# Loading the first batch's keys and queries as six consecutive rows of a head, and transposing them on two corners of the TensorE array

## The chip, the cores and the metric

The kernel runs on one core of a Trainium2 chip. The metric is the device time of one execution in microseconds (us). A core has TensorE (matrix products, PE in the profile, its weight loads PEld), VectorE (DVE), ScalarE (ACT), GpSimd (POOL) and SyncE (SP, which here only issues transfers), and 16 DMA engines that move data between the device memory and the on-chip memory. The on-chip memory has 128 partitions; what TensorE reads or writes also lies across partitions.

## The reference

Attention over 4 batches, 8 heads, 768 positions and 64 elements a head, with two kinds of heads, and then a feed-forward layer on its result.

```python
scores = scale * np.matmul(q, k.transpose(0, 1, 3, 2))      # q, k: (4, 8, 768, 64), float32
causal = rel >= 0                                           # rel = query position - key position
stream_keep = causal & (is_sink | in_win)                   # first 4 keys, or a window of 64
mask = np.where(retr, full_mask, stream_mask)               # retrieval heads 0, 2, 6: all earlier keys
a = softmax(np.where(mask, scores, -1e9))
attn = np.matmul(a, v)                                      # then to x: (3072, 512)
h = np.maximum(np.maximum(x @ w1, x @ w2), x @ w3)          # w: (512, 768)
return h @ w_out                                            # (768, 512)
```

## The kernel before

The order of all the work is written out by hand: `PROGRAM` (L84 to L150) is a list of small steps, and each engine carries out its instructions in the order in which these steps issue them. An engine whose next instruction waits holds up everything behind it.

The work goes by batch and, within one, by halves of 384 positions. For each half there are scores (a matrix product of keys and queries into PSUM, then the exponential on ACT into `pt`), masks, the product with the values (`av`), a turn of the result (`xT`), the hidden layer (`f`, L439) and the output (`o`, L464). Batches 1 to 3 take their keys and queries by GpSimd loads that cast on the way (`load`, L261) and turn them with VectorE (L275). Batch 0 is different, and it alone is touched by the change. Its path is:

- `load_pairs` (L198): one transfer for the keys and one for the queries of a pair of heads and a half of the positions, 192 KB each, as float32. There are four pairs and two halves, so 16 transfers. Partition p takes rows 3p to 3p + 2 of both heads of the pair: 3 x 64 floats of a head are 768 consecutive bytes. `hl` steps call it, and the first two pairs are loaded ahead of the program (L314, L315). SP issues 13 of the transfers, ACT 3.
- `cast_pair` (L216, step `cast`): a cast to float16 for the keys (`kn`) and one for the queries (`qn`), by the engine that the step names (d is VectorE, a ScalarE, p GpSimd). It also changes the order from head-row-element to row-head-element.
- `turn_pair` (L228, step `turnp`): TensorE transposes the 128 x 128 block of each j (row in a partition's three) into a PSUM bank `tr`, three for the keys and three for the queries. One or two copies (L241) bring them into `KQ`, sorted by position; head 0 of the pair lies on partitions 0 to 63, head 1 on 64 to 127.
- `first_scores` (L589, step `s0`) uses `KQ`.

The queues around it. SP issues its transfers in order, and from the ninth on a transfer waits for the landing of the one eight before it, since there are eight completion counters (DMAHW0 to 7) for the transfers of SP and ACT together. The staging buffers of three of the groups of pairs (`pairs2`) are two deep, so the third group also waits for casts of the first. The program's lines that bear on the order:

```python
"idle 11, hl 0 2 2 s cs, cast 0 1 pd, turnp 0 1 aa, cast 0 0 dd, cast 0 2 dp, load_v 0 0 0 4 s",
"s0 0 0 3, vc 0 0 4 p, vc 0 4 4 p, s0 0 0 1, kx0 0 2 p, s0 0 0 2, hl 1 2 2 s s, cast 1 0 dd",
"turnp 1 0 dd, load 1 0 0, cast 1 1 pp, w 0, load 1 0 1, cast 1 3 dp, vt 0 02 da, cast 1 2 aa",
"vt 0 1 a, turnp 1 1 d, y 0 0 1:4:2 r p, s0 0 1 2, s0 0 1 3, y 0 0 4:5:1 r r, turnp 1 3 ad",
```

In `load 1 0 0` and `load 1 0 1` GpSimd issues the keys and queries of batch 1, in `w 0` the first weight matrix (L400).

Of the kernel before, what the change touches and what calls it, by code (L numbers as in the profile page):

```python
# [9 lines left out]
FP16 = mybir.dt.float16  # L10
FP32 = mybir.dt.float32
# [5 lines left out]
PAIRS = ((0, 2), (1, 3), (4, 6), (5, 7))  # L17
# [136 lines left out]
def fast(ctx, tc, keep, q, k, v, is_retrieval, n_sink, window, moe_w1, moe_w2, moe_w3, moe_w_out, w_t, woutt, out):  # L154
    nc = tc.nc
    B, H, S, D = q.shape
    DMdl = out.shape[1]
    DF = moe_w1.shape[1]
    P = 128
# [4 lines left out]
    HALF = S // 2  # L164
    HB = HALF // P
# [9 lines left out]
    pairs2 = ctx.enter_context(tc.tile_pool(name="pairs2", bufs=2))  # L175
    once = ctx.enter_context(tc.tile_pool(name="once", bufs=1))
    third = ctx.enter_context(tc.tile_pool(name="third", bufs=2))
    half16 = ctx.enter_context(tc.tile_pool(name="half16", bufs=3))
# [11 lines left out]
    def bank(shape, dtype, name):  # L190
        return bkp.tile(shape, dtype, tag="bank", name=name)
# [4 lines left out]
    staged, cast, KQs, landed = {}, {}, {}, {}  # L196

    def load_pairs(half, hp, n, engines):  # L198
        for nm, src, eng in zip(("ks", "qs"), (k, q), engines):
            st = (  # L200
                pairs2.tile([P, 4, HB, D], FP32, tag=nm, name=nm) if n == 2
                else once.tile([P, 2 * n, HB, D], FP32, name=f"{nm}{hp}")
            )
            for h in range(0, 2 * n, 2):
                h0, h1 = PAIRS[hp + h // 2]
                eng[h // 2].dma_start(  # L206
                    out=st[:, h : h + 2],
                    in_=src[0, h0 : h1 + 1 : h1 - h0, half * HALF : (half + 1) * HALF].rearrange(
                        "h (p j) d -> p h j d", p=P
                    ),  # L210
                )
            for i in range(n):
                staged.setdefault((half, hp + i), []).append(st[:, 2 * i : 2 * i + 2])
                landed[half, hp + i] = st[0:1, 2 * i, 0, 0:2]

    def cast_pair(half, hp, engines):  # L216
        cast[half, hp] = []
        for nm, src, op in zip(("kn", "qn"), staged.pop((half, hp)), engines):
            x = half16.tile([P, HB, 2, D], FP16, tag=nm, name=nm)
            op(out=x, in_=src.rearrange("p h j d -> p j h d"))  # L220
            cast[half, hp].append(x)

    def of_pair(hp):
        return KQs[0, hp // 2].rearrange("p i t two -> p i (t two)")[
            :, hp % 2
        ].rearrange("p (i t) -> p i t", i=2)

    def turn_pair(half, hp, *engines):  # L228
        if (0, hp // 2) not in KQs:
            KQs[0, hp // 2] = qkt.tile([P, 2, S, 2], FP16, tag="KQ", name="KQ")  # L230
        xs = cast.pop((half, hp))
        n = 2 // len(engines)
        for part, op in enumerate(engines):
            tr = bank([P, 1024], FP16, "tr")
            for i in range(n):
                for j in range(HB):
                    c = i * HALF + j * P
                    nc.tensor.transpose(
                        tr[:, c : c + P], xs[part + i][:, j].rearrange("p h d -> p (h d)"), ident
                    )  # L240
            op(  # L241
                out=of_pair(hp)[
                    :, part : part + n, half * HALF : (half + 1) * HALF
                ].rearrange("p i (t j) -> p i t j", j=HB),
                in_=tr[:, 0 : n * HALF].rearrange("p (i j t) -> p i t j", i=n, j=HB),
            )

    def load(b, quad, *which):
# [61 lines left out]
    def load_first(half, hp, n, *e):  # L310
        by = {"s": nc.sync, "c": nc.scalar}
        load_pairs(half, hp, n, [[by[x] for x in y * n][:n] for y in e])
# [10 lines left out]
    def idle_work(n):  # L323
# [11 lines left out]
        out=kb[:, 2:4], in_=kb[:, 2:4], compare_op=ALU.is_ge, fill=0.0,  # L335
# [3 lines left out]
        out=kb[:, 3], in_=kb[:, 3], compare_op=ALU.is_gt, fill=0.0,  # L339
# [3 lines left out]
        out=kb[:, 1:5:3], in_=kb[:, 1:5:3], compare_op=ALU.is_gt, fill=0.0,  # L343
        base=window - P, pattern=[[0, 2], [-1, P]], channel_multiplier=1,
    )
    ident = consts.tile([P, P], FP16, name="ident")
# [4 lines left out]
        out=every3, in_=every3, compare_op=ALU.not_equal, fill=1.0,  # L351
# [4 lines left out]
    if n_sink > 0:  # L356
# [4 lines left out]
        out=far, in0=kb[:, 0:5], scalar1=FAR, scalar2=-FAR, op0=ALU.mult, op1=ALU.add  # L361
# [346 lines left out]
    xs = {}  # L708
# [35 lines left out]
    def turn_x(b, half, hp, op):  # L744
        x = xs.pop((b, half, hp))
        tr = bank([P, 1024], FP16, "tr")
        for i in range(HB):
            nc.tensor.transpose(  # L748
                tr[:, i * P : (i + 1) * P], x[:, i].rearrange("p h d -> p (h d)"), ident
            )  # L750
        op(out=xT[b, half, hp].rearrange("p a t -> p (a t)"), in_=tr[:, 0:HALF])
# [55 lines left out]
    def reduce_one(out, in_):  # L807
# [12 lines left out]
        f=lambda b, half, wi, ni, *e: hidden(int(b), int(half), int(wi), int(ni), *[ops[x] for x in e]),  # L820
# [7 lines left out]
        x=lambda b, half, hp, e: turn_x(int(b), int(half), int(hp), ops[e]),  # L828
# [223 lines left out]
```

## Time and profile before

| | us |
|---|---|
| median of 3 runs | 187.92 (187.65 to 189.06) |
| the profiled execution | 187.55 |
| its span, first to last instruction | 186.1 |
| PE, DVE, ACT, POOL busy in the span | 178.6, 144.9, 99.4, 82.8 |
| PE busy in the first 30 us | 27.6 (the 2 us rows of the windows view, added) |

The profile's times are those of one execution. A matmul's end is modelled, so that short matmuls issued back to back overlap in the rows; their spacing is read from a group's length. The DMA share of a window is the mean over 16 engines, and can pass 1 a little where packets overlap. A row of the timeline gives the start, the duration, the engine, the line, the operation, what it writes and reads, and how many of the kind stand together.

### The profile page before, as it was taken

Reading aid. Unit: us, or ns where it says so; the run is one execution under the profiler, and the core shown is the slowest. Engines: PE = TensorE matmul, PEld = TensorE weight load, DVE = VectorE, ACT = ScalarE, POOL = GpSimd, SP = SyncE. Lnnn points to the kernel's source line nnn. Section 1 sums busy time; section 2 is a strip of 40 time slices with the busy share of each in tenths; the row PEclk is TensorE's granted clock in tenths of the full one; section 3 lists DMA queues with packets and bytes.
Section 4 is the critical chain, followed back from the end, with each engine's and each line's share of the span. In section 5 each row is a group of like instructions: output and inputs, shape, how many; then the busy total and the mean of one; then the engine's idle time right before and its main releaser. Section 6 shows DMA issues by size and latency. Waiting matters only on the chain.

```text
span 186.1 us, 4755 instructions
## 1 busy us (share of the span) xinstructions
PE 178.6 (96%) x1863; PEld 105.5 (57%) x1863; DVE 144.9 (78%) x308; ACT 99.4 (53%) x161; POOL 82.8 (44%) x142
## 2 busy tenths in 40 slices
PE   6889999999999999999999999999999999999992
PEld 2455646566656456765555566655655575555551
DVE  3659997989899977888979899765883699475553
ACT  3399998378955648687096336665446301311110
POOL 7498998809883990299057002126313400000000
PEclk9999999999999999999999999999999999999999
DMA  5999999999899999349593301321133013401404
GB/s 157 318 328 291 212 209 209 212 236 220 165 143 163 170 269 212 79 105 221 142 258 90 113 0 56 67 81 56 27 65 113 0 60 63 139 2 56 167 19 161
DMA packets 43005, 26.30 MB, mean 141 GB/s; under 512 B 29794, under 2 KB 38498, under 8 KB 42978
## 3 DMA queue, kind: packets, MB, share of 16 engines
q1 hardware_dynamic: 37826, 17.44, 36.4%
q0 software_dynamic: 4192, 7.87, 23.3%
q10 hardware_dynamic: 960, 0.66, 1.2%
q8 instruction: 15, 0.25, 0.5%
q14 instruction: 12, 0.10, 0.2%
HBM read 25.17 MB, written 6.29 MB: 169 GB/s over the span
## 4 chain that ended last, share of the span: by engine, by line
PE 85%; DVE 7%; DMA 3%; ACT 2%; SPq 1%; issue 1%; DVEq 0%; ACTq 0%
PE yy L439 47%; PE yy L464 15%; PE oacc L725 8%; PE st L682 7%; PE yst L439 3%; DMA qs<-in_q_dram 3%; DVE KQ L241 2%; PE yst L464 1%; DVE KQ L275 1%; SPq L206 1%; ACT pt L637 1%; DVE x L732 1%; DVE vx L808 1%; PE st L616 1%; PE vb L513 1%; PE tr L748 1%
## 5 line engine op out<-in xcount | busy, mean ns | idle before, releaser
L379 POOL TENSOR_TENSOR pt<-pt,kb 128x512 f16<-128x512 f16 (+5 forms) x53 | 48.3, 932 | 59.3 <-ACT pt L699 50.4
L699 ACT ACTIVATE pt<-st 128x1024 f16<-128x1024 f32 (+2 forms) x51 | 43.5, 908 | 24.9 <-PE st L682 24.5
L439 PE MATMUL yy<-xT,w2t 128*128 128x384 f16 x184 | 36.2, 326 | 0.0
L439 PE MATMUL yy<-xT,w0t 128*128 128x384 f16 x180 | 34.5, 326 | 0.0
L439 PE MATMUL yy<-xT,w1t 128*128 128x384 f16 x176 | 34.2, 326 | 0.0
L464 PE MATMUL yy<-woutt,hT 128*128 128x512 f16 (+1 forms) x138 | 31.4, 372 | 0.0
L451 DVE TENSOR_TENSOR hT<-yy,acc 128x384 f16<-128x384 f32 x46 | 25.2, 556 | 5.0 <-PE yy L439 3.3
L451 DVE TENSOR_TENSOR acc<-yy,acc 128x384 f16<-128x384 f32 x44 | 24.0, 556 | 5.8 <-PE yy L439 4.2
L275 DVE STREAM_TRANSPOSE KQ<-kq 128x384 f32<-128x384 f32 x24 | 25.3, 1132 | 1.0 <-POOL pt L379 1.0
L439 PEld LDWEIGHTS <-w0t 128*128 128x128 f16 x192 | 18.1, 98 | 12.5 <-issue 0.4
L447 ACT CAST acc<-yy 128x384 f16<-128x384 f32 x27 | 12.9, 491 | 22.7 <-PE yy L439 20.6
L439 PEld LDWEIGHTS <-w1t 128*128 128x128 f16 x192 | 17.8, 98 | 11.9 <-issue 0.6
L439 PEld LDWEIGHTS <-w2t 128*128 128x128 f16 x192 | 17.7, 98 | 11.8 <-issue 0.2
L464 PEld LDWEIGHTS <-hT 128*128 128x128 f16 x150 | 14.4, 98 | 15.3
L473 ACT COPY ot<-yy 128x512 f32<-128x512 f32 (+1 forms) x14 | 7.9, 566 | 21.4 <-PE yy L464 18.9
L725 PEld LDWEIGHTS <-pt 128*128 128x128 f16 x472 | 17.2, 97 | 3.6 <-issue 0.6
L725 PE MATMUL oacc<-va,pt 128*128 128x65 f16 x392 | 18.6, 193 | 0.2 <-DVE pt L379 0.2
L732 DVE TENSOR_TENSOR x<-oacc,sums 128x384 f16<-128x384 f32 x32 | 17.8, 558 | 1.1
L637 ACT ACTIVATE pt<-st 128x1024 f16<-128x1024 f32 (+5 forms) x22 | 15.4, 767 | 0.4 <-PE st L616 0.2
L682 PE MATMUL st<-KQ 32*128 32x128 f16 (+2 forms) x342 | 15.1, 257 | 0.0
L379 DVE TENSOR_TENSOR pt<-pt,kb 128x256 f16<-128x256 f16 (+4 forms) x31 | 12.3, 401 | 1.8 <-ACT pt L699 1.7
L447 DVE CAST acc<-yy 128x384 f16<-128x384 f32 x18 | 10.0, 559 | 3.4 <-PE yy L439 3.0
(119 smaller groups left out, 190.7 us busy)
## 6 DMA issues: line engine op xcount, KB each, us to landing
out_dram<-ot SPq DMA_DIRECT2D x23, 256.0 KB, 2.0
vs<-in_v_dram SPq DMA_DIRECT2D x18, 256.0 KB, 4.9
ks<-in_k_dram SPq DMA_DIRECT2D x8, 192.0 KB, 5.9
kq<-in_k_dram POOLq DMA_DIRECT2D x3, 384.0 KB, 7.7
kq<-in_q_dram POOLq DMA_DIRECT2D x3, 384.0 KB, 9.3
qs<-in_q_dram SPq DMA_DIRECT2D x5, 192.0 KB, 5.4
kq<-in_k_dram POOLq DMA_DIRECT2D x3, 288.0 KB, 6.0
kq<-in_q_dram POOLq DMA_DIRECT2D x3, 288.0 KB, 7.1
```

What stands on the lines that cost most here:

```text
L275: nc.vector.transpose(out=dst.rearrange("c (p j) -> c j p", j=n)[:, j0:j1], in_=src.rearrange("c (j i) -> c j i", i=R),)
L379: engine.tensor_tensor(out=x, in0=x, in1=of_blocks(kb, pattern, rows), op=ALU.mult)
L439: nc.tensor.matmul(yy[:, 0:HALF], w_t[wi][:, ks, ni * P : (ni + 1) * P], xT[b, half, ks].rearrange("p a t -> p (a t)"), start=(ks == 0), s ...
L447: op(out=acc[b, half, ni], in_=yy[:, 0:HALF])
L451: nc.vector.tensor_tensor(out=acc[b, half, ni] if wi == 1 else hT[b, half, ni], in0=yy[:, 0:HALF], in1=acc[b, half, ni], op=ALU.max,)
L464: nc.tensor.matmul(yo[:, 0:n], hT[b, half, ns][:, tb * P : (tb + 1) * P], woutt[:, ns, c : c + n], start=(ns == 0), stop=(ns == NNB - 1),)
L473: op(out=ot[:, c : c + n], in_=yo[:, 0:n])
L637: nc.scalar.activation(out=pts[0, half, hp, u][:, r0:r1, c0:c1], in_=sts[hp][:, r0:r1, c0:c1], func=AF.Exp, scale=sc,)
L682: nc.tensor.matmul(sts["XY"[g // 2]][:, g % 2, c0 : c0 + n * P], KQ[rows, 0, ki * P : (ki + 1) * P] if kind == "p" else kx[b % 2][quad][ro ...
L699: nc.scalar.activation(out=pts[b, s, xy][:, r0:r1, c0:c1], in_=st[:, r0:r1, c0:c1], func=AF.Exp, scale=sc,)
L725: nc.tensor.matmul(o[:, i, r, 0 : D + 1], at[b, h, kind, ki, qi], vv[:, 0 : D + 1], start=(n == 0), stop=(n == len(todo) - 1), skip_group_ ...
L732: nc.vector.tensor_tensor(out=x, in0=o[:, :, :, 0:D], in1=rc.unsqueeze(3).to_broadcast([P, HB, 2, D]), op=ALU.mult,)
```

## The change

The transfer now gives a head of the pair to each half of the partitions. Partition p of the lower half takes rows 6p to 6p + 5 of the first head, and partition 64 + p those of the second, so that 6 x 64 floats, 1536 consecutive bytes, are one piece. The number of transfers, their bytes, their order and the issuing engines stay. The source pattern now has the head outermost, then 64 groups of rows, then 384 floats: `h p (j d)` in place of `p h j d`. The cast no longer reorders. A transposition takes a 64 x 64 block: for each of six rows j, one on partitions 0 to 63 into the columns of the same number and one on partitions 64 to 127, by `tile_position`. The copy into `KQ` gathers six rows in place of three. Lines from L220 on carry a number 1 lower, at L238 1 higher and from L241 on 2 higher.

```diff
     def load_pairs(half, hp, n, engines):
         for nm, src, eng in zip(("ks", "qs"), (k, q), engines):
             st = (
-                pairs2.tile([P, 4, HB, D], FP32, tag=nm, name=nm) if n == 2
-                else once.tile([P, 2 * n, HB, D], FP32, name=f"{nm}{hp}")
-            )
-            for h in range(0, 2 * n, 2):
-                h0, h1 = PAIRS[hp + h // 2]
-                eng[h // 2].dma_start(
-                    out=st[:, h : h + 2],
+                pairs2.tile([P, 2, 2 * HB, D], FP32, tag=nm, name=nm) if n == 2
+                else once.tile([P, n, 2 * HB, D], FP32, name=f"{nm}{hp}")
+            )
+            for i in range(n):
+                h0, h1 = PAIRS[hp + i]
+                eng[i].dma_start(
+                    out=st[:, i].rearrange("p j d -> p (j d)"),
                     in_=src[0, h0 : h1 + 1 : h1 - h0, half * HALF : (half + 1) * HALF].rearrange(
-                        "h (p j) d -> p h j d", p=P
+                        "h (p j) d -> h p (j d)", p=P // 2
                     ),
                 )
-            for i in range(n):
-                staged.setdefault((half, hp + i), []).append(st[:, 2 * i : 2 * i + 2])
-                landed[half, hp + i] = st[0:1, 2 * i, 0, 0:2]
+                staged.setdefault((half, hp + i), []).append(st[:, i])
+                landed[half, hp + i] = st[0:1, i, 0, 0:2]
 
     def cast_pair(half, hp, engines):
         cast[half, hp] = []
         for nm, src, op in zip(("kn", "qn"), staged.pop((half, hp)), engines):
-            x = half16.tile([P, HB, 2, D], FP16, tag=nm, name=nm)
-            op(out=x, in_=src.rearrange("p h j d -> p j h d"))
+            x = half16.tile([P, 2 * HB, D], FP16, tag=nm, name=nm)
+            op(out=x, in_=src)
             cast[half, hp].append(x)
...
             for i in range(n):
-                for j in range(HB):
-                    c = i * HALF + j * P
-                    nc.tensor.transpose(
-                        tr[:, c : c + P], xs[part + i][:, j].rearrange("p h d -> p (h d)"), ident
-                    )
+                for j in range(2 * HB):
+                    c = i * HALF + j * D
+                    for r in range(2):
+                        rows = slice(D * r, D * r + D)
+                        nc.tensor.transpose(
+                            tr[rows, c : c + D], xs[part + i][rows, j], ident[rows, rows],
+                            tile_position=(rows.start, rows.start),
+                        )
             op(
                 out=of_pair(hp)[
                     :, part : part + n, half * HALF : (half + 1) * HALF
-                ].rearrange("p i (t j) -> p i t j", j=HB),
-                in_=tr[:, 0 : n * HALF].rearrange("p (i j t) -> p i t j", i=n, j=HB),
+                ].rearrange("p i (t j) -> p i t j", j=2 * HB),
+                in_=tr[:, 0 : n * HALF].rearrange("p (i j t) -> p i t j", i=n, j=2 * HB),
             )
```

How the order stands. SP's queue before, from its first value load to the last of the keys and queries (`vs` values, `ks` keys, `qs` queries, with the number of the buffer, and what the issue waits for):

```order
L298 DMA vs_202<-in_v_dram 128x4x192 [waits DMAHW0_49]
L298 DMA vs_202<-in_v_dram 128x4x192 [waits DMAHW1_49]
L206 DMA ks_244<-in_k_dram 128x2x192 [waits DMAHW2_49]
L206 DMA ks_244<-in_k_dram 128x2x192 [waits DMAHW3_49]
L206 DMA qs_247<-in_q_dram 128x2x192 [waits DMAHW4_49]
L206 DMA qs_247<-in_q_dram 128x2x192 [waits DMAHW5_49]
L206 DMA ks_322<-in_k_dram 128x2x192 [waits DMAHW6_49,DVE_49,Pool_49]
L206 DMA ks_322<-in_k_dram 128x2x192 [waits DMAHW7_49]
L206 DMA qs_325<-in_q_dram 128x2x192 [waits DMAHW0_49,Activation_49]
L206 DMA qs_325<-in_q_dram 128x2x192 [waits DMAHW1_49]
```

And the same place after:

```order
L300 DMA vs_220<-in_v_dram 128x4x192 [waits DMAHW0_49]
L300 DMA vs_220<-in_v_dram 128x4x192 [waits DMAHW1_49]
L206 DMA ks_280<-in_k_dram 128x1x384 [waits DMAHW2_49]
L206 DMA ks_280<-in_k_dram 128x1x384 [waits DMAHW3_49]
L206 DMA qs_283<-in_q_dram 128x1x384 [waits DMAHW4_49]
L206 DMA qs_283<-in_q_dram 128x1x384 [waits DMAHW5_49]
L206 DMA ks_394<-in_k_dram 128x1x384 [waits DMAHW6_49,DVE_49,Pool_49]
L206 DMA ks_394<-in_k_dram 128x1x384 [waits DMAHW7_49]
L206 DMA qs_397<-in_q_dram 128x1x384 [waits DMAHW0_49,Activation_49]
L206 DMA qs_397<-in_q_dram 128x1x384 [waits DMAHW1_49]
```

No transfer moved and no wait was added; a partition's part is one run of 384 floats where it was two of 192. The size shown is that of the destination.

On TensorE, before, the end of the second pair's transposes and the start of the first scores (`ident` is the identity, `far` a mask block):

```order
L238 LDWEIGHTS qn
L238 MATMUL tr<-ident,qn 128x128
L601 LDWEIGHTS ident
L601 MATMUL st<-far,ident 128x128
L601 LDWEIGHTS ident
L601 MATMUL st<-far,ident 128x128
L616 LDWEIGHTS KQ
L616 MATMUL st<-KQ 128x128
```

And after, at the same place:

```order
L239 LDWEIGHTS qn
L239 MATMUL tr<-ident,qn 64x64
L603 LDWEIGHTS ident
L603 MATMUL st<-far,ident 128x128
L603 LDWEIGHTS ident
L603 MATMUL st<-far,ident 128x128
L618 LDWEIGHTS KQ
L618 MATMUL st<-KQ 128x128
```

The order of the kinds is the same; ahead of this place a turn of keys or queries has twelve pairs of such rows in place of three, so that TensorE has 288 rows more in all (192 transposes in place of 48).

On GpSimd, whose order is the same before and after, the place where the second half's casts stand between loads that it issues (before):

```order
L505 CAST vn<-vs 128x768 [waits DMAHW1_49]
L566 COPY kx_155<-KQ 128x2x64 [waits DVE_49]
L571 COPY kx_155<-KQ 128x4x4
L261 DMA kq<-in_k_dram 128x1536
L220 CAST kn<-ks 128x384 [waits DMAHW3_49,PE_49,Pool_49]
L220 CAST qn<-qs 128x384 [waits DMAHW5_49,PE_49,Activation_49]
L400 DMA w0t<-in_moe_w_dram 128x4x768
L261 DMA kq<-in_q_dram 128x1536
L220 CAST qn<-qs 128x384 [waits DMAHW1_49,PE_49]
```

Nothing moved here: batch 1's keys, the first weights and batch 1's queries are issued between casts that wait for batch 0's transfers.

## The prediction

> **What bounds the kernel now.** I read the page first, its busy times and its DMA slices.
>
> ```profile
> span 186.1 us, 4755 instructions
> ...
> PE 178.6 (96%) x1863; PEld 105.5 (57%) x1863; DVE 144.9 (78%) x308; ACT 99.4 (53%) x161; POOL 82.8 (44%) x142
> ...
> DMA  5999999999899999349593301321133013401404
> ```
>
> TensorE bounds the whole, but not the part that the change touches. The change is in the first 17 us, where the DMA engines are full, and there I asked for windows and for the start of the chain in order of time.
>
> ```profile
> 0.00:2.00 2.00, 0.50 (x2) 0.23 (x3) 0.29 (x3) 0.00 (x0) 1.09 (x6) 1.00 0.00 0
> 2.00:4.00 2.00, 2.00 (x6) 0.67 (x5) 1.20 (x5) 1.49 (x2) 1.86 (x6) 1.00 0.90 267
> ```
>
> ```profile
> 6.00:12.00 6.00, 4.90 (x51) 2.96 (x51) 4.28 (x12) 4.50 (x10) 4.30 (x12) 1.00 1.08 337
> 16.00:30.00 14.00, 12.78 (x188) 8.12 (x187) 13.57 (x30) 13.50 (x26) 13.04 (x22) 1.00 1.13 220
> ```
>
> The columns are PE, PEld, DVE, ACT, POOL busy, the granted clock, the DMA share and GB/s. Data moves from about 2.1 us on, all 16 DMA engines are busy, and together they bring 337 GB/s. From 16 to 30 us PE idles for only 1.2 us of 14. So what comes after 16 us runs at the pace of the engines, and what comes before waits for batch 0's keys and queries:
>
> ```profile
> 3.10 5.57 DMA qs<-in_q_dram
> ...
> 8.74 0.51 ACT qn L220
> ```
>
> This is the longest single piece of the chain before 28 us: the fourth pair's queries hold back cast, transposition and scores. The last of the 16 transfers is seen on GpSimd, whose cast of the queries of pair 3, second half, waits for it:
>
> ```profile
> 16.01 0.51 POOL L220 CAST qn<-qs 128x384 f16<-128x384 f32 x1 [0.54 <-DMA qs<-in_q_dram]
> ```
>
> At 16.0 us, then, batch 0's queries are complete. In TensorE's order the transposes of that pair, of pair 2 behind it, and all later work stand behind this cast; on GpSimd the second weight load stands behind it. If 16.0 becomes a later time, nearly everything after it moves by the same amount, for PE has hardly any idle time there to give back.
>
> **The transfers, and over how many engines they go.** Every transfer here is cut up among DMA engines. Before, both sides of a key or query transfer count 128 outermost (128 groups of rows, 128 partitions). After, the source counts 2 outermost (the heads), the destination still 128. To give an engine its share, the issuing side must cut both patterns at the same bytes, and the simplest cut is along the outermost count of each; a number of shares that divides 128 and 2 is 2. I take this: a transfer of the changed kernel goes over 2 of the 16 engines, the same two each time, one head each. No row of the trace shows a transfer whose two outermost counts differ, so this is a mechanism of this kernel's patterns, and its alternative (16 shares by the destination's partitions) is a rival below.
>
> The Trainium skill, page "DMA: Bandwidth & Descriptors", section "Why a DMA increments its semaphore by 16 and not by 1", has the rule: the number of engines is the largest up to 16 that divides both patterns' slowest dimension that is not 1, and for SP and ACT these are the lowest-numbered ones. By that rule it is 2 here, and the sum is the one that follows; by the trace, where all engines are full at 337 GB/s, it would stay near 187.
>
> What does a packet of 1536 bytes take an engine? Two rows of the DMA view lie around it, q1 being SP's queue (packets, MB, share of the 16 engines), from 6 to 12 us and from 168 to 176 us:
>
> ```profile
> q1 hardware_dynamic: 2633, 1.93, 103.2%
> ```
>
> ```profile
> DMA packets 432, 0.79 MB, mean 98 GB/s; under 512 B 48, under 2 KB 48, under 8 KB 432
> ...
> q1 hardware_dynamic: 432, 0.79, 26.2%
> ```
>
> In the first, 103.2% of 16 x 6 us are 99 us for 2633 packets, of 733 bytes in the mean and nearly all of 768: 38 ns each. In the second only results are stored, 2048 bytes a packet: 26.2% of 16 x 8 us are 33.5 us for 384 of them, 87 ns. On the line between the two, 1536 bytes take 68 ns. The ends are 65 ns (1536/2048 of 87) and 76 ns (twice 38).
>
> ```profile
> ks<-in_k_dram SPq DMA_DIRECT2D x8, 192.0 KB, 5.9
> kq<-in_k_dram POOLq DMA_DIRECT2D x3, 384.0 KB, 7.7
> ...
> vs<-in_v_dram SPq DMA_DIRECT2D x2, 384.0 KB, 5.8
> ...
> w0t<-in_moe_w_dram POOLq DMA_DIRECT2D x1, 768.0 KB, 10.1
> ```
>
> In these rows stand the sizes (KB each) and the time from issue to landing. A transfer of 192 KB is 128 packets, 64 on each of two engines: 64 x 68 ns = 4.35 us. Sixteen are 1024 packets an engine, 69.6 us. The pair is not left without work in between: SP and ACT have eight transfers out, all of them keys and queries at the start, and each landing lets one more be issued. The wait of the third group of pairs for casts of the first is met at about 2.1 + 8 x 4.35 = 37 us, while four transfers of the second group are still queued.
>
> The same two engines also carry a sixteenth each of what others load meanwhile. The first half's values, 0.79 MB, lie in the same queue: 0.79 MB at 337 GB/s, 2.3 us. GpSimd's loads of batch 1's keys and queries and of the first weights stand in its order ahead of the last cast, so they come in before the last queries, not after:
>
> ```profile
> 12.51 0.75 POOL L261 DMA_DIRECT2D kq<-in_k_dram  x1
> ...
> 14.17 0.78 POOL L400 DMA_DIRECT2D w0t<-in_moe_w_dram  x1
> ```
>
> ```profile
> q0 software_dynamic: 1410, 2.48, 111.5%
> ```
>
> From 18 to 30 us GpSimd's queue q0 took 111.5% of 16 x 12 us, 214 us, for 2.48 MB. The three loads are 1536 KB, 1.57 MB: 136 us, 8.5 us on each engine. The bounds are 4 (half of it overlaps) and 8.5.
>
> The landing itself: queries of the first pair, issued at 1.05, land 3.0 us later (the shortest in the second row below, for `qs`), 4.05; 2 x 192 KB at 337 GB/s from 2.1 on are over at 3.3; so 0.8 us for the end of a transfer.
>
> ```profile
> 1.05 1.04 ACTq L206 DMA_DIRECT2D qs<-in_q_dram  x2
> ```
>
> ```profile
> DMA to landing us min/median/max: 3.0/4.2/5.4
> ```
>
> The last queries land at 2.1 + 69.6 + 2.3 + 8.5 + 0.8 = 83.3 in place of 16.0: 67.3 us later. The stall at 3.10 goes into this; it isn't added.
>
> **Casts, transposes, copies.** Only those behind the last landing are on the path: one cast, the transposes and copies of pairs 3 and 2.
>
> ```profile
> 16.41 0.34 PE L238 MATMUL tr<-ident,kn 128*128 128x128 f16 x3
> ```
>
> ```profile
> 28.31 1.39 PE oacc L725 x39
> ```
>
> ```profile
> L238 PE MATMUL tr<-ident,kn x24: 219/219/230, 6.2 to 17.9; 128*128 128x128 f16 x24
> ...
> L241 DVE COPY KQ<-tr x9: 540/557/948, 7.8 to 18.8; 128x384 f16<-128x384 f16 x8, 128x768 f16<-128x768 f16 x1
> ...
> L751 DVE COPY xT<-tr x3: 347/347/358, 22.8 to 23.4; 128x384 f16<-128x384 f16 x3
> ```
>
> Three transposes of 128 columns take 0.34 us with the last one's 0.219, so 60 ns apart; the smallest matmuls in the trace, 65 columns, are 1.39 / 39 = 36 ns apart. A turn of a pair had 6 x 60 = 0.36 us and gets 24 x 36 = 0.86: +0.5. At best the two corners run side by side, 12 x 36 = 0.43, +0.1. Two turns cost +0.2 to +1.0; pair 2's keys and most of pair 3's are turned early, so I take +0.5. (By the Trainium skill, page "TensorEngine Tiling (Array Packing)", section "Key Properties", different tiles run in parallel: that is the +0.1 end; the 36 ns row is from whole-array matmuls and can't decide it.) The copies keep size and a stride of 128 or 64 elements; a gather takes 557 ns, an ordered copy 347, so -0.2 to +0.2 each, and I take 0. The cast, 0.51 us, becomes a plain one: 0, -0.2 at best.
>
> TensorE will have waited for most of 80 us. At its first start the matmuls of 512 columns lie further apart than later:
>
> ```profile
> 1.50 4.38 PE L326 MATMUL idl<-zero 128*128 128x512 f16 x11 [1.50 <-DVE warm L329]
> ```
>
> ```profile
> 86.92 1.29 PE yy L464 x6
> ```
>
> That is 0.40 against 0.215 us, over 4.4 us. If this comes again at 83 us it costs up to 4.4 x 0.46 = 2.0, otherwise 0; 1.0. Some small work that was late at 16 us will have been done by then; PE's idle 1.2 us after 16 is the most that this can give, and I take a quarter, -0.3.
>
> Sum against the profiled execution: 187.55 + 67.3 + 0.5 + 1.0 - 0.3 = 256.05, so **256**. The median of the runs is 0.4 above the profiled one, within their spread.
>
> **Rivals.** (a) Sixteen engines, cut by the destination's partitions. For it: every transfer now reaches 337 GB/s with 128 partitions on the chip's side, and that side stays. A transfer is then 8 packets of 68 ns an engine in place of 16 of 38: 0.06 us less, 1.0 over sixteen; plus the two turns' +0.5: 187.0, **not slower**. It decides as soon as the first keys land before 6 us. (b) Sixteen engines, but TensorE pays: eight turns x 0.5 = 4.0, less the 1.0, with little of it inside the waits: 190.5. Against it: before 16 us PE waits for data. (c) Two engines a transfer, but another two each time. Eight in flight then fill all 16; only the first keys are late, 2.1 + 4.35 + 0.8 = 7.25 against the cast at
>
> ```profile
> 5.61 0.50 POOL L220 CAST kn<-ks 128x384 f16<-128x384 f32 x1 [0.96 <-DMA ks<-in_k_dram]
> ```
>
> so 1.6 later: 189.2. (d) The change doesn't do what it says: the packets stay at 768 bytes on two engines, 128 x 38 ns = 4.9 us a transfer, 77.8 in all, 8.2 more than in the sum: 264. It belongs to the forecast's range.
>
> **The numbers.** Two fixed engines, (d) included: 0.86. (a) 0.07, (b) 0.03, (c) 0.04. I go so high because two unequal outermost counts leave a simple cutter no other common share, and 2 to 16 engines has no middle. Low end: 65 ns (-3.1), GpSimd's loads at 4 (-4.5), no slow restart (-1.0), PE's idle time gone (-1.2), and rounding: 245. High end: 76 ns (+8.2), slow restart in full and turns in full (+1.5), and gaps in the pair's queue of some 2 us: 268. About 0.80 lies inside. One per cent, 1.9 us, is what a measurement can tell. Faster by more: 0.01 (of (a)); within: 0.09 (rest of (a), 0.03 of (c)); slower: 0.90.
>
> **What would show it.** In the profile of the changed kernel the DMA share should be near 2/16 for 80 us, with some 45 GB/s (2 x 1536 bytes in 68 ns); keys and queries should take 9 us and more from issue to landing; the last cast of `qn` on GpSimd should start near 83 us, and from there on the chain should read as it does from 16 us on, 170 us long. Transposes are 192. If the first landing is at 5 to 6 us with the share at 9 tenths, the two engines were wrong, and with them the whole sum; if the share is 2/16 but the last cast is at 75 or 90, the packet's time or GpSimd's share of the pair was.

## The result, and the profile after

The changed kernel took **251.34 us** (median of 4 runs, 250.97 to 251.62), the kernel before 188.38 (187.65 to 189.06, 4 runs beside it): a ratio of 1.336, with a 95% interval of 1.331 to 1.340. The forecast was 256, in a range of 245 to 268. The profiled execution took 251.23 us, its span is 249.6. Ratios here and below are worked out without one run of the first experiment, over 1.5% longer than the fastest of its kernel, which counts as a slow run.

The page of the kernel after: span, TensorE's busy time, the granted clock and the DMA engines in 40 slices of 6.2 us, and the shares of the chain.

```profile
span 249.6 us, 5043 instructions
...
PE 187.2 (75%) x2007; PEld 110.0 (44%) x2007; DVE 144.1 (58%) x308; ACT 99.9 (40%) x161; POOL 83.0 (33%) x142
...
PE   7004119052003999999999999999999999999994
...
PEclk9755555757555799999999999999999999999999
DMA  0111324117451989976999478830131140140133
...
PE 66%; DMA 15%; SPq 14%; DVE 2%; ACT 1%; issue 0%; POOL 0%; DVEq 0%; POOLq 0%
```

TensorE's line of the kernel before, in slices of 4.65 us:

```profile
PE   6889999999999999999999999999999999999992
```

From the fourteenth slice on TensorE is as busy as before from the fourth on. What is new is the time ahead of it: 13 slices with the DMA engines mostly at one to four tenths and TensorE mostly idle. The windows of the same kernel (columns: PE, PEld, DVE, ACT, POOL busy, granted clock, DMA share, GB/s) give the numbers.

```profile
6.00:12.00 6.00, 0.04 (x1) 0.00 (x0) 0.00 (x0) 0.00 (x0) 0.00 (x0) 0.75 0.13 50
...
78.00:82.00 4.00, 2.94 (x55) 2.10 (x57) 2.33 (x5) 1.30 (x2) 3.38 (x8) 0.50 0.07 22
84.00:90.00 6.00, 5.85 (x68) 3.24 (x66) 5.13 (x12) 5.49 (x9) 4.91 (x7) 0.99 1.13 214
```

In the stretch in which 337 GB/s came before, 50 come now, at a DMA share of 0.13, which is two engines of 16. The DMA view from 4 to 16 us counts the packets: all but four of them have 1536 bytes.

```profile
DMA packets 391, 0.59 MB, mean 50 GB/s; under 512 B 4, under 2 KB 391, under 8 KB 391
...
q10 hardware_dynamic: 209, 0.32, 7.2%
q1 hardware_dynamic: 182, 0.28, 6.1%
```

Two engines for 12 us are 24 us of engine time; divided by 391 packets that is 61.4 ns a packet, or 25 GB/s an engine. The timeline of GpSimd has the cast that stood at 16.01 us before:

```profile
78.50 0.51 POOL L219 CAST qn<-qs 128x384 f16<-128x384 f32 x1 [20.50 <-DMA qs<-in_q_dram]
```

Batch 0's queries are complete 62.5 us later. From there to the end of the span it is 171.1 us; before it was 186.1 - 16.0 = 170.1. So the loss of 63.5 us of span is 62.5 us of waiting for these transfers and 1.0 us behind them.

### The profile page after: what moved, and what is told of

The parts are those of the page before. It is cut to its first block, busy times and chain, and to the rows that moved or that the text cites. A ratio compares the mean times of both kernels' runs of the same rounds, so it can differ in the third digit from the quotient of the medians.

```text
span 249.6 us, 5043 instructions
## 1 busy us (share of the span) xinstructions
PE 187.2 (75%) x2007; PEld 110.0 (44%) x2007; DVE 144.1 (58%) x308; ACT 99.9 (40%) x161; POOL 83.0 (33%) x142
## 4 chain that ended last, share of the span: by engine, by line
PE 66%; DMA 15%; SPq 14%; DVE 2%; ACT 1%; issue 0%; POOL 0%; DVEq 0%; POOLq 0%
PE yy L441 35%; DMA qs<-in_q_dram 15%; SPq L206 12%; PE yy L466 11%; PE oacc L727 7%; PE st L684 5%; PE yst L441 2%; SPq L300 2%; PE st L618 1%; PE vb L515 1%; PE yst L466 1%; DVE KQ L277 1%; PE tr L239 1%; PE tr L750 0%; ACT pt L639 0%
## 5 line engine op out<-in xcount | busy, mean ns | idle before, releaser
L466 PE MATMUL yy<-woutt,hT 128*128 128x512 f16 (+1 forms) x138 | 31.4, 372 | 0.0
L239 PE MATMUL tr<-ident,kn 64*64 64x64 f16 x96 | 4.1, 236 | 31.9 <-POOL kn L219 18.8
L441 PEld LDWEIGHTS <-w1t 128*128 128x128 f16 x192 | 17.8, 98 | 11.9 <-issue 0.6
L727 PE MATMUL oacc<-va,pt 128*128 128x65 f16 x392 | 19.4, 198 | 0.3 <-DVE pt L381 0.2
L727 PEld LDWEIGHTS <-pt 128*128 128x128 f16 x472 | 18.0, 100 | 3.7 <-issue 0.6
L239 PE MATMUL tr<-ident,qn 64*64 64x64 f16 x96 | 4.0, 234 | 20.6 <-DVE qn L219 9.2
L734 DVE TENSOR_TENSOR x<-oacc,sums 128x384 f16<-128x384 f32 x32 | 17.8, 558 | 1.1
L239 PEld LDWEIGHTS <-kn 64*64 64x64 f16 x96 | 3.3, 147 | 34.3 <-POOL kn L219 19.8
L219 DVE CAST kn<-ks 128x384 f16<-128x384 f32 x4 | 1.4, 358 | 29.1 <-DMA ks<-in_k_dram 29.1
```

Source lines behind the costliest of these rows:

```text
L239: nc.tensor.transpose(tr[rows, c : c + D], xs[part + i][rows, j], ident[rows, rows], tile_position=(rows.start, rows.start),)
L441: nc.tensor.matmul(yy[:, 0:HALF], w_t[wi][:, ks, ni * P : (ni + 1) * P], xT[b, half, ks].rearrange("p a t -> p (a t)"), start=(ks == 0), s ...
L466: nc.tensor.matmul(yo[:, 0:n], hT[b, half, ns][:, tb * P : (tb + 1) * P], woutt[:, ns, c : c + n], start=(ns == 0), stop=(ns == NNB - 1),)
L727: nc.tensor.matmul(o[:, i, r, 0 : D + 1], at[b, h, kind, ki, qi], vv[:, 0 : D + 1], start=(n == 0), stop=(n == len(todo) - 1), skip_group_ ...
L734: nc.vector.tensor_tensor(out=x, in0=o[:, :, :, 0:D], in1=rc.unsqueeze(3).to_broadcast([P, HB, 2, D]), op=ALU.mult,)
```

## The experiments

Each time below is compared with runs of the kernel before on the same chip: 188.05 us for one transfer a head, 2 outermost, half the packet and GpSimd's loads behind; 188.15 for four and eight outermost, twice as many transfers and the first version with sixteen; 187.84 for the values earlier and the next two versions; 188.03 for the last one. "Last cast" is GpSimd's cast of pair 3's queries, second half: 16.0 us before, 78.5 after.

### One transfer a head

The theory that the two outermost counts (2 heads, 128 partitions) confine a transfer to two engines is tested by taking the 2 away. Packets, layout and turns stay.

```diff
-                eng[i].dma_start(
-                    out=st[:, i].rearrange("p j d -> p (j d)"),
-                    in_=src[0, h0 : h1 + 1 : h1 - h0, ...].rearrange("h (p j) d -> h p (j d)", p=P // 2),
-                )
+                for r, h in enumerate((h0, h1)):
+                    eng[i].dma_start(
+                        out=st[D * r : D * r + D, i].rearrange("p j d -> p (j d)"),
+                        in_=src[0, h, half * HALF : (half + 1) * HALF].rearrange("(p j) d -> p (j d)", p=P // 2),
+                    )
```

> The changed kernel with one transfer a head (64 rows on 64 partitions, both sides count 64 outermost), so 32 transfers of 96 KB; packets of 1536 bytes, casts and transposes stay as changed. Theory (two engines because the source counts two heads outermost): all 16 engines carry each transfer again, DMA share 0.9 and more from 3 us on, the last cast of qn starts at 16 to 20 us, time 188 to 193 us. Rival (long packets, the halves of the partitions or the small transposes are what is slow): near 251 us.

It took 199.48 us (median of three executions, 198.50 to 201.22; ratio 1.061, 1.051 to 1.070). The fourth, which is the profiled one, took 205.61; its last cast stands at 23.4 us:

```profile
23.43 0.51 POOL L220 CAST qn<-qs 128x384 f16<-128x384 f32 x1 [2.67 <-DMA qs<-in_q_dram]
```

52 of the 63 us come back, so the pattern of the transfers was the cause, and not the packets, the layout or the turns. But 11 us stay lost, where I had expected 0 to 5. That is followed up further below. (As the profiled execution took some 6 us longer than the others, single waits of its profile are not to be weighed to the microsecond.)

### One head a transfer, but a 2 outermost in the source

```diff
-                            "(p j) d -> p (j d)", p=P // 2
+                            "(b a j) d -> a b (j d)", a=2, b=P // 2 // 2
```

> As the run with one transfer a head, but the source of a transfer counts 2 outermost (row groups of even and of odd number; the positions of batch 0's keys and queries then stand in another order, so its attention is of other positions). Theory: two engines a transfer, 1024 packets of 1536 bytes on each, 249 to 258 us. Rival (it was having two heads in a transfer, not the count): as the run with one transfer a head.

251.43 us. The timeline of GpSimd:

```profile
78.89 0.51 POOL L220 CAST qn<-qs 128x384 f16<-128x384 f32 x1 [20.55 <-DMA qs<-in_q_dram]
```

With 32 transfers of one head each the loss is all there again, to 0.4 us. So it isn't two heads in a transfer, nor two halves of the partitions, but the count of 2 that stands outermost in the source.

### Four and eight outermost

The same with `a=4` and `a=8`.

> One transfer a head, the source counting 4 outermost (every fourth row group together; batch 0's positions then stand in another order, so its attention is of other positions). Theory (as many engines as the two outermost counts share): 4 engines, 512 packets of 62 ns on each, 31.7 us; last cast of qn at 2.1 + 31.7 + 2.3 + 8.5 + 0.8 = 45 us, time 214 to 224 us. Rival (any source pattern of three levels is slow, whatever its count): as with a count of 2, 251 us.

> The same with the source counting 8 outermost (positions again in another order). Theory: 8 engines, 256 packets of 62 ns on each, 15.9 us; last cast of qn at 28 to 34 us, time 200 to 208 us. Rival (three levels are slow): 251 us.

220.62 us and 203.25 us, both inside the ranges of the theory. The last casts, and the DMA views early in the load (4 to 12 us, and 4 to 10 us), first for four:

```profile
47.36 0.51 POOL L220 CAST qn<-qs 128x384 f16<-128x384 f32 x1 [12.46 <-DMA qs<-in_q_dram]
```

```profile
DMA packets 549, 0.79 MB, mean 99 GB/s; under 512 B 32, under 2 KB 549, under 8 KB 549
```

and for eight:

```profile
29.58 0.51 POOL L220 CAST qn<-qs 128x384 f16<-128x384 f32 x1 [7.52 <-DMA qs<-in_q_dram]
```

```profile
DMA packets 740, 1.02 MB, mean 170 GB/s; under 512 B 78, under 2 KB 740, under 8 KB 740
```

The rate goes 50, 99, 170 GB/s with 2, 4 and 8. 1024 packets of 61.4 ns on each of two engines are 62.9 us; on four half of that, on eight a quarter. The steps to be expected are so 31.4 and 15.7 us; the last casts step by 31.5 (78.9 to 47.4) and 17.8 (47.4 to 29.6), the second 2.1 us more than expected. Each was executed once, which is enough for steps of this size. By the Trainium skill, page "DMA: Bandwidth & Descriptors", section "Why a DMA increments its semaphore by 16 and not by 1", the number of engines is the largest up to 16 that divides both outermost counts; these runs agree for 2, 4 and 8.

### Half the packet

Is part of the loss the longer packet? Here each transfer keeps the changed kernel's pattern over the heads, but brings three of the six rows, 768 bytes a packet, and there are twice as many.

```diff
-                eng[i].dma_start(out=st[:, i]...
+                for j0 in (0, HB):
+                    eng[i].dma_start(out=st[:, i, j0 : j0 + HB]...
```

> The changed kernel with each transfer cut in two, three of the six rows each: packets of 768 bytes as before the change, source still with two heads outermost. Theory: two engines, 2048 packets an engine at 36 to 38 ns in place of 1024 at 62, so 10 to 14 us more than the changed kernel: 261 to 266 us. Rival (the packet of 1536 bytes is what is slow): near 190 us.

257.72 us, 6.4 more than the changed kernel where I had expected 10 to 14: slower, as the theory has it, but below its range. The last cast comes 6.1 us later than with the long packets. GpSimd's timeline, and the DMA view from 4 to 16 us:

```profile
84.65 0.51 POOL L220 CAST qn<-qs 128x384 f16<-128x384 f32 x1 [21.76 <-DMA qs<-in_q_dram]
```

```profile
DMA packets 703, 0.53 MB, mean 44 GB/s; under 512 B 8, under 2 KB 703, under 8 KB 703
```

24 us / 703 = 34 ns for 768 bytes, where I had taken 36 to 38, against 61 for 1536: the long packet saves 7 ns in 68. That is what the change gains by its packets, and it is a tenth of the engines' time.

### GpSimd's loads behind the last cast

The sum had 8.5 us for three loads of GpSimd that pass over the same two engines ahead of the last queries. Two of them, w0 and batch 1's queries (1152 of 1536 KB, so 6.4 us of the 8.5), are moved behind the cast:

```diff
-    "..., cast 1 1 pp, w 0, load 1 0 1, cast 1 3 dp, vt 0 02 da, ...",
+    "..., cast 1 1 pp, cast 1 3 dp, w 0, load 1 0 1, vt 0 02 da, ...",
```

> The changed kernel with GpSimd's load of the first weights and of batch 1's queries issued behind the casts of pair 3, not ahead of them. Theory (these loads took their sixteenth of the two engines' time from the keys and queries, 6.5 of the 8.5 us in the sum): last cast of qn at about 72 us in place of 78.5, 245 us. Rivals: they overlapped with the keys and queries at no cost, 251 us; or the weights now come too late for the hidden layer, 251 to 256 us.

247.95 us (247.60 and 248.30), 3.4 us less than the change. The timeline of GpSimd, and TensorE's first scores behind the cast:

```profile
72.80 0.51 POOL L219 CAST qn<-qs 128x384 f16<-128x384 f32 x1 [16.00 <-DMA qs<-in_q_dram]
73.28 0.78 POOL L402 DMA_DIRECT2D w0t<-in_moe_w_dram  x1
...
74.06 0.54 POOL L263 DMA_DIRECT2D kq<-in_q_dram  x1
74.64 0.40 POOL L534 COPY vx<-va 64x256 f16<-64x256 f16 x1
...
75.45 0.29 PE L618 MATMUL st<-KQ,kx 64*128 64x128 f16 x2 [1.13 <-POOL kx L568]
```

The cast comes 5.7 us earlier, near the 72 us expected: the term was about right. But the time is 3 us above the 245 expected, and the span is only 3.6 us shorter (246.0). Of the 2.1 us given back, 1.3 are seen here: the two issues, 1.32 us, now stand between the cast and GpSimd's copies, and those hold the scores, which start 2.65 us after the cast, against 1.38 in the kernel after (79.88 - 78.50).

### The kernel before, with twice as many transfers

Where do the 11 us of the first experiment go? It has 32 transfers of 96 KB in place of 16 of 192 KB. Here the kernel before, with its packets, its layout and its turns, gets the same number:

```diff
+                for r, x in enumerate((h0, h1)):
                     eng[h // 2].dma_start(
-                        out=st[:, h : h + 2], in_=src[0, h0 : h1 + 1 : h1 - h0, ...]
+                        out=st[:, h + r], in_=src[0, x, ...]
                     )
```

> The kernel before with each transfer of a pair cut into one a head: 32 transfers of 96 KB, packets of 768 bytes, 128 outermost on both sides, casts and transposes as before. Theory (the run with one transfer a head lost its 12 us by the number of transfers: with eight out at a time half as many bytes are on the way, and the second half's values come up later in SP's queue): 196 to 203 us. Rival (it lost them by the small transposes or the long packets): 188 to 190 us.

197.78 us (ratio 1.050, 1.046 to 1.055). So twice as many transfers alone cost 9.6 us, most of what the first experiment lost. SP's last issues of queries, first in the kernel before and then here, and GpSimd's last cast show how:

```profile
9.92 1.54 SPq L206 DMA_DIRECT2D qs<-in_q_dram  x2
```

```profile
14.79 1.95 SPq L207 DMA_DIRECT2D qs<-in_q_dram  x4
```

```profile
24.44 0.51 POOL L219 CAST qn<-qs 128x384 f16<-128x384 f32 x1 [7.83 <-DMA qs<-in_q_dram]
```

The last transfers of queries are issued 5 us later, when GpSimd's loads have begun, and land 8 us later. The engines are less full, too: in windows of 4 us from 4 to 16 us the DMA share is 0.86, 0.96 and 0.88, against 1.02, 1.09 and 1.10 in the kernel before. I take it that with a fixed number of transfers out at a time half the size means half the bytes under way; the runs show the later issues and the lower share, not that cause.

### The values earlier

In the first experiment's profile TensorE waited longest for the second half of the values, whose load SP issues behind all keys and queries. Here it is issued ahead of the last two pairs.

```diff
-    "..., s0 0 0 2, hl 1 2 2 s s, cast 1 0 dd",
+    "..., s0 0 0 2, load_v 0 1 s, hl 1 2 2 s s, cast 1 0 dd",
```

> One transfer per head as in the first experiment (200.35 us), with the load of the values' second half issued on SyncE ahead of the last two pairs' keys and queries of the second half in place of behind them. In the first experiment TensorE stood idle from about 31 to 39 us for GpSimd's cast of these values, whose transfer was issued at 20.1 us and took 17 us beside GpSimd's loads. Theory, that late transfer is most of the first experiment's loss: 190 to 194. Rival, the loss is the 32 transfers and goes elsewhere (the last queries land later instead): 197 to 201.

201.56 us (201.05 to 202.11; ratio 1.071): the theory fell, and the time is just above the rival's range too. (The 200.35 us of the expectation are the median of all four runs of the first experiment, the longest included.) The windows of this kernel, and GpSimd's last cast:

```profile
20.00:28.00 8.00, 0.53 (x12) 0.51 (x12) 2.11 (x4) 1.92 (x6) 0.00 (x0) 0.62 1.14 270
```

```profile
28.46 0.51 POOL L220 CAST qn<-qs 128x384 f16<-128x384 f32 x1 [10.08 <-DMA qs<-in_q_dram]
```

All engines are full (1.14) and TensorE has next to nothing to do: now the last queries are late, 5.0 us later than in the first experiment's profile (28.46 against 23.43). The long wait for the values, on the other hand, stood in a profile of 205.61 us. In that of the kernel before with as many transfers GpSimd's cast of these values, at 29.60 us, doesn't wait for them at all. So the theory rested on a wait of one execution, an unusually long one; whether the shorter ones had it no run shows.

### Sixteen transfers with 128 outermost

Can the long packet be had without either loss? A whole head has 768 rows, six for each of 128 partitions. So a transfer is one head, 192 KB, 1536 bytes a packet, 128 outermost on both sides, and there are 16 as before. A cast is then 768 elements long, and a corner's transposes take their input from the partitions of one half: `tile_position` is (64 * half, 64 * head). As each transfer brings both halves, the program's first lines had to be put in another order.

```diff
+                for r, h in enumerate(PAIRS[hp + i]):
+                    eng[i].dma_start(
+                        out=st[:, r].rearrange("p j d -> p (j d)"),
+                        in_=src[0, h].rearrange("(p j) d -> p (j d)", p=P),
+                    )
```

> The change's idea without the two engines: one transfer brings a head's 768 rows, six consecutive rows of 1536 bytes to each of 128 partitions, both sides counting 128 outermost, 16 transfers of 192 KB as before. The lower half of the partitions is then the first half of the positions; a head of a pair goes to its half of the partitions by the transposes (two corners in one row of the array). A cast takes a pair's keys or queries whole, so eight casts in place of sixteen, and the steps are put in an order that takes the second half of pairs 0 and 1 ahead of pairs 2 and 3. Theory: all queries at 12 to 14 us, DMA share 0.9 and more from 3 us, 185 to 189 us. Rival (the 192 small transposes cost what the loads save): 189 to 193 us.

196.48 us (ratio 1.044, 1.042 to 1.047): above both ranges, a miss. Its windows:

```profile
4.00:8.00 4.00, 2.38 (x30) 1.02 (x28) 2.47 (x2) 0.95 (x4) 3.24 (x8) 1.00 0.99 330
8.00:12.00 4.00, 2.69 (x37) 1.64 (x38) 2.27 (x7) 1.33 (x4) 0.83 (x1) 0.52 0.94 307
...
16.00:20.00 4.00, 1.89 (x38) 1.19 (x38) 3.52 (x7) 0.90 (x2) 1.38 (x4) 0.80 0.35 107
20.00:24.00 4.00, 4.00 (x24) 1.38 (x23) 0.34 (x1) 2.42 (x4) 3.62 (x6) 0.50 0.27 31
```

The engines are full from the start, but not from 16 to 24 us: in my order GpSimd's loads stand too far behind. And the granted clock falls to a half. Three more versions try these one after the other.

First matmuls of zeros where TensorE waited between 6 and 9 us:

```diff
+            if (half, hp, part) == (0, 1, 1):
+                idle_work(4)
...
-    "turnp 0 1 aa, cast 0 dd, ...",
+    "turnp 0 1 aa, idle 4, cast 0 dd, ...",
```

> Whole heads as before (the 16-transfer version, 196.5 us), plus eight matmuls of zeros that nobody reads: four between the first pair's turn of keys and its turn of queries, four behind it, where TensorE waited 1.2 and 1.4 us. In that version the granted clock stood at 0.50 to 0.85 from 8 to 28 us. Busy time times (1 - clock) over these stretches is 2.69*0.48 + 3.70*0.37 + 1.89*0.20 + 4.00*0.50 + 4.00*0.15 = 5.6 us of TensorE work that a full clock would not have needed; the other 3.5 us of its loss are idle time. Theory: the clock fell because TensorE stood idle from 6.4 to 9.3 us, and the fall itself costs most of the loss: 191 to 193.5, granted clock 1.0 up to 15 us at least. Rival: TensorE waits for casts and loads there whatever its clock: 195.5 to 197.

```profile
12.00:16.00 4.00, 1.99 (x70) 1.33 (x68) 2.17 (x4) 2.03 (x3) 0.00 (x0) 1.00 0.92 291
16.00:20.00 4.00, 3.02 (x45) 1.47 (x46) 2.14 (x5) 1.14 (x3) 2.81 (x6) 0.68 0.54 173
20.00:24.00 4.00, 4.00 (x21) 1.49 (x19) 0.69 (x1) 2.67 (x4) 2.19 (x4) 0.50 0.58 98
```

196.12 us, inside the rival's range. The clock held up to 16 us, as the windows show, and nearly nothing came of it: TensorE then waited for most of 14.5 to 17 us instead, and the clock fell at 17.5. Of my 5.6 us, 2.7 were for 8 to 16 us (2.69*0.48 + 3.70*0.37); the full clock there gave 0.4. The sum had counted work at a low clock as lost where TensorE would have waited anyway. Second, the order as well:

```diff
-    "idle 11, hl 3 1 s s, hl 2 1 s s, load_v 0 0 0 4 s, load_v 0 0 4 4 s, load_v 0 1 s, cast 1 pd",
+    "idle 11, hl 3 1 s s, load_v 0 0 0 4 s, hl 2 1 s s, load_v 0 0 4 4 s, load_v 0 1 s, cast 1 pa",
...
+    "load 1 0 0, s0 0 1 1, s0 0 0 0, idle 1, turnp 0 3 da, clear 0 d, s0 0 1 0, kx0 0 3 p",
+    "w 0, s0 0 0 3, vc 0 0 4 p, cast 2 dd, turnp 0 2 da, load 1 0 1, vc 0 4 4 p, s0 0 0 1",
```

> The same with the eight matmuls, and the first stage in another order: values half 0 loaded between the third and the fourth pair's keys and queries, GpSimd's loads of batch 1's keys, of w0 and of batch 1's queries issued ahead of its casts of the values (in the version before they were issued at 21.6 to 23.6 us and the DMA engines stood empty from 18 to 24 us; in the kernel before the change at 12.5 to 15.5 us), the turns of the second half behind those of the first, and four buffers for the casts in place of three. Theory, what the 16-transfer version lost is order and clock and not its layout: 187 to 191. Rival, whole heads bring the first half of all pairs too late, since twice the bytes land ahead of it: 193 to 197.

194.50 us (193.37 to 195.38; ratio 1.032), a miss by 3.5 us for the theory and inside the rival's range. The engines are now full up to 24 us. The granted clock of the profiled execution was low from 12.4 to 22.6 us, so third, seven more matmuls of zeros, at 9.1 and 14.3 us (`idle 4` becomes `idle 6`; `idle 5` ahead of `turnp 0 2 da`):

> The 16-transfer version in its second order (194.5 us), with seven more matmuls of zeros: two ahead of the second pair's turn (TensorE idle 0.37 us there, from 9.1) and five ahead of the fourth pair's turn of the first half (idle 0.80 us, from 14.3). There the granted clock fell at 12.7 us and came back near 22; TensorE was busy without a gap from 16 to 24 us at 0.50 and 0.67, so that a full clock would have saved 3.04*0.45 + 4.00*0.50 + 4.00*0.33 = 4.7 us of its work. Theory, the fall of the clock is what is left of the loss, and the two short idle times bring it: the clock stays at 1.0 and the time comes to 189.5 to 191.5. Rival, the loads and casts set that stretch whatever the clock (as the first attempt with filler suggests, which gained 0.4 us): 193 to 195.5.

```profile
8.00:16.00 8.00, 7.51 (x116) 3.79 (x114) 4.92 (x12) 4.66 (x8) 5.33 (x10) 1.00 1.03 329
16.00:24.00 8.00, 7.87 (x186) 5.12 (x183) 5.91 (x13) 6.98 (x12) 4.49 (x12) 1.00 1.12 218
```

193.36 us (191.96 to 194.57; ratio 1.029, 1.026 to 1.033): 1.9 us above the theory's range and inside the rival's. The clock stayed at 1.0, and the profiled execution, 191.96, is 3.4 us under the last one's 195.38; the medians differ by 1.1 only, within the spread of the two. The four executions of the second order say more of the clock: two had a mean granted clock of 0.97 and took 195.38 and 195.19 us, two had 0.99 and 1.00 and took 193.37 and 193.81. So I estimate the clock's part at some 1.7 us of the 6.7 that were lost; with a full clock the last two versions take about the same time. What holds the other 5 us is open. None of the versions with long packets beats the kernel before.

## Why the prediction was right

**The engines (right).** The step "a transfer goes over 2 of the 16 engines, the same two each time" is what the runs show: a share of 0.13; 78.9 us with one head and a count of 2; 47.4 with 4; 29.6 with 8; 23.4 with 64. Rivals (a) and (b), 16 engines, and (c), another two each time, are excluded by the 50 GB/s with several transfers out at once, and (d), packets of 768 bytes, by the packets of 1536 in the DMA view.

**The packet (mis-sized).** This is the term of the sum that failed: 68 ns, 61.4 measured, 1024 x 6.6 = 6.8 us too much. The measured packet lies even below the 65 ns that the range took for its low end. Two things in its working were wrong. A share of 103.2% counts packets that overlap, so 38 ns for 768 bytes should have been 16 x 6 / 2633 = 36; the run with small packets on two engines has 34. And the other point of the line was a store's packet of 2048 bytes; two loads of 768 bytes (68 ns) would have been the upper end and not the middle.

**Values and GpSimd's loads (about right as far as tested).** 2.3 and 8.5 us. Of the 8.5, 6.4 were put to the test and gave 5.7; the rest, and the 2.3 of the values, were not. With 61.4 ns the sum for the last landing is 2.1 + 62.9 + 2.3 + 8.5 + 0.8 = 76.6, and 78.5 was measured; the remaining 1.9 us are not assigned. They offset part of the 6.8 us of the packet, so that the whole came out closer than its largest wrong term; that much was luck. So the last cast was predicted at 83.3 and came 4.8 us earlier, which is nearly all of the 4.8 us between 256.05 and the profiled 251.23.

**Behind the last cast (+1.2 forecast, +1.0 measured).** The tile view of `qn` has the parts:

```profile
L239 PE MATMUL tr<-ident,qn x96: 192/237/259, 22.3 to 80.8; 64*64 64x64 f16 x96
L219 DVE CAST qn<-qs x3: 353/359/360, 18.2 to 52.2; 128x384 f16<-128x384 f32 x3
L219 POOL CAST qn<-qs x3: 506/507/507, 26.3 to 78.5; 128x384 f16<-128x384 f32 x3
L219 ACT CAST qn<-qs x2: 511/512/512, 36.2 to 74.6; 128x384 f16<-128x384 f32 x2
```

The cast on the path is GpSimd's, and a plain source changes nothing for it; VectorE's is 0.36 in place of 0.55 us, off the path. 96 transposes of queries and as many of keys are the 192. The turn's copies are as they were (557 ns on VectorE, 492 on ScalarE), as assumed. The slow restart came: the clock stood at 0.50 from 78 to 84 us. The transposes were taken too dear: with all engines loading and at full clock (first experiment) two groups of twelve start 0.21 us apart,

```profile
7.57 0.38 PE L240 MATMUL tr<-ident,kn 64*64 64x64 f16 x12 [1.19 <-POOL kn L220]
7.78 0.35 PE L240 MATMUL tr<-ident,qn 64*64 64x64 f16 x12
```

so a turn of 24 is about 0.4 us and not 0.86. That is 17 ns a transposition, less than half of the 36 ns between the smallest whole-array matmuls: the two corners run side by side, the +0.1 end of the estimate. Behind the last cast itself the clock was at 0.50, and two such groups start 0.34 us apart (at 80.20 and 80.54 us). How the +1.0 divides between the turns and the slow clock the runs don't show, so the total came out, and its parts are not confirmed.

**What the signs did.** Share, last cast within 5 us, the tail of 170 us and the 192 transposes came as written. The times from issue to landing can't be read: the page gives none for these transfers.

## What to carry to other kernels

Count the outermost dimension of both sides of a transfer before anything else: a small count there (heads, groups) takes engines away from it in proportion (2, 4 and 8 were tried), and longer packets, 10% here, don't make up for it. Taking the small count away by cutting the transfer into more has its own price, 9.6 us here for 32 in place of 16. Moving the load of the values ahead of queries in a full queue made the queries late here. And a wait that is seen in a single profile should be looked for in the other executions before a change is built on it.

## What the hardware showed beside this

**An issue that can't go is held at the issuing engine.** SP's first row in the kernel before, and its rows in the kernel after:

```profile
1.05 2.00 SPq L206 DMA_DIRECT2D ks<-in_k_dram  x4
```

```profile
1.05 16.71 SPq L206 DMA_DIRECT2D ks<-in_k_dram  x4
17.80 6.48 SPq L206 DMA_DIRECT2D qs<-in_q_dram  x1
```

Four issues took 2.00 us before and 16.7 here. ScalarE's queue was held for 4.0 us too, at 2.86. The chain of waits therefore puts 14% to SP's queue and 15% to the transfers, though both are the same two engines. I had thought of the waiting as one in the landing alone, with eight transfers issued ahead; by 17.8 us only seven had been issued, four by SP and three by ScalarE. The two engines had work all the same (a share of 0.13 from 4 to 16 us), so the sum is not touched by it.

**TensorE's clock.** In the kernel after it idles from 6.0 us; the granted clock falls at about 9 (0.75 in the mean from 6 to 12 us, above, is a full clock for half of it and 0.50 for the rest). It works again from 79.1 us and has its full clock near 84, some 5 us later. Windows of 0.1 and 0.2 us place all changes of the clock in this trace: down at 9.0, up at 43.1, down at 46.5, up at 56.8, down at 60.2 and up at 84.1 us. The distances between them, 34.1, 3.4, 10.2, 3.4 and 23.9 us, are 10, 1, 3, 1 and 7 times 3.41: the clock changed only at points of a fixed grid of 3.41 us. By the Trainium skill, page "TensorE: Matmul & The Clock Gate", section "Part 1: The HAM clock gate (the "warmup" mystery)", half the clock is the state after an idle stretch of about 3.4 us, and a busy stretch of that length ends it; the length agrees, and so do the 5 us if the stretches are counted from the points of the grid. But a stretch need not be idle throughout: TensorE was still at work in the first 0.5 us of the one that ended in the fall at 9.0, and for 1.2 us of the one that ended at 60.2. (In the first 4 us the granted clock reads 1.00 before and after the change, while the matmuls there lie about 0.4 us apart against 0.215 later; it doesn't show the state at the start.)

In the profiled execution of the sixteen-transfer kernel in its second order the clock fell at 12.4 us and came back at 22.6, again three times 3.41 us later. TensorE's timeline there has no longer idle time behind its first matmul than 0.42 us:

```profile
6.46 0.38 PE L241 MATMUL tr<-ident,kn 64*64 64x64 f16 x12 [0.42 <-POOL kn L218]
...
9.44 0.37 PE L241 MATMUL tr<-ident,kn 64*64 64x64 f16 x12 [0.37 <-DVE kn L218]
...
12.39 0.39 PE L620 MATMUL st<-KQ 64*128 64x256 f16 x2
12.72 1.03 PE L605 MATMUL st<-far,ident 128*128 128x512 f16 x2
```

The row at 12.39 is the first at the low clock; the last row has two matmuls in 1.03 us where they take 0.59 at full clock. In the 3.4 us ahead of the fall TensorE idled for less than 0.5 us in all. The rule of the idle stretch doesn't explain it, and no run here does.
